# The first microseconds of a layer norm, windowed attention and gated FFN kernel: load order, statistics engine, early tiles and placement of the attention-value runs

## The chip, the cores and the metric

The kernel runs on one core of one Trainium2 chip. The metric is device time in microseconds (us) for one execution. The time before is the median of three runs; one further execution was profiled, and its trace is what the prediction reads.

## The reference

The input x has 2048 rows of 576 features, in bf16. The reference, cut to what matters:

```python
xn = layernorm(x)                            # per row, eps = 1e-5
qkv = xn @ wqkv                              # 576 x 1728; 32 heads of 18
scores = q @ k.T * 18 ** -0.5                # causal, window of 256 keys
s = (softmax(masked scores) @ v) @ wo        # 576 x 576
h = sigmoid(xn @ w_gate) * (xn @ w_up)       # 576 -> 4608
g = silu(h @ w_down)                         # 4608 -> 576
out = x + s * g
```

## The kernel before

**Tiling.** The rows are cut into four chunks of 512 (`NC`), and each chunk into four blocks of 128 rows (`BPC`). A chunk has its layer norm (`build_ln`), its query, key and value projections, attention in eight groups of four heads (`build_attn`), the product with the attention's output matrix (`build_wo`), and the FFN (`build_ffn`): 36 F tiles of 128 columns with gate and up together, called f1, and then the down products, called f2. Contractions of 64 rows run as two matmuls at a time, one in the upper and one in the lower half of the array; "a pair" below is such a couple. The 576 features are 64 (the remainder, held in `wgr`) and four times 128 (in `wgs`). One F tile is a lo half of 4 pairs, which needs `wgs` of gate and of up, and a hi half of 5 pairs, which needs `wgr` as well. A hi half waits for its lo half.

**Order.** Every engine runs a list of operations that a planner in the program (`schedule`) writes out from estimated durations, priorities and memory that comes free. TensorE is filled throughout: FFN tiles are put between the scores of the attention (`space`), so that the exponentials keep up. The FFN uses PSUM units 2, 3 and 1 (`pool_f`), scores, transposes and projections 0 and 1 (`pool_s`). The attention-value products come in eight runs, two to a chunk (`build_pv`), each of 256 (chunk 0) or 384 very short TensorE instructions with all four PSUM units held. `fits` lets a run start only where, by the plan, a stretch of TensorE's instruction list (pages of 256 instructions) has taken long enough before it (`FETCH_NS`).

**The opening.** All loads are issued by SyncE (SP) one after the other: four x blocks, then gate and up columns of the first two F tiles (weights group 0), then the remainder rows for four F tiles, then weights group 1, and so on. Meanwhile TensorE runs matmuls on zeros (`warm`: 43 pairs, and 10 more after the first transposes). For blocks 0, 1 and 3, VectorE takes the sums (L541, L543), aggregates them (L545), adds eps (L547), GpSimd raises to the power of -1/2 (L549), VectorE applies (L557) and copies 64 columns (L561), TensorE transposes (L613), and ScalarE, or VectorE for block 3, copies the result into `xnT` (L590). For block 2 the sums are taken on ScalarE in two passes (L600, L602), with a GpSimd step after each (L601, L603).

**Early tiles.** The first two F tiles (`NEARLY`) are cut by block into four parts of 128 rows, so that TensorE can start on a block as soon as it is there; the lo half of the third tile, whole, runs before the last part's hi half (`ahead`). Three lines that the change rewrites:

```python
pr = 1 + wg if c == 0 and wg < 4 else 3
ahead = self.pool_f.hold()
if edge > at and when(edge) - when(edge - FETCH - FETCH_AHEAD) < FETCH_NS[ffn]:
    return False
```

Of the kernel before, what the change touches and what calls it, by code (L numbers as in the profile page):

```python
# [21 lines left out]
FG = 4  # L22
# [23 lines left out]
FETCH_NS = (6200.0, 4350.0)  # L46
RUN_NS = 6.3
STEP_NS = (54.0, 30.6)
# [20 lines left out]
LN_PRIO = (0, 0, 0, 16)  # L69
X_PRIO = (0, 0, 0, 0)  # L70
REM_PRIO = 0.6
STATS_ACT = (2,)
APPLY_ACT = ()
DUP_ACT = ()
XE_ENG = ("ACT", "ACT", "ACT", "DVE")
NWARM = (43, 10)
NEARLY = 2
FIRST_SLACK_NS = (-800.0, -1500.0)
BUSY_SLACK_NS = 1500.0
PARTS = (((0, 1), (1, 2), (2, 3), (3, 4)),) * NEARLY  # L80
# [10 lines left out]
POOL_IN_NS = 140.0  # L91
DMA_PE_NS = 690.0
FILL_NS = 100.0
SPACE_NS = (1700, 1800, 1700, 1700)
# [8 lines left out]
def act_ns(n):  # L103
    return n / 1.2 + 175.0
# [52 lines left out]
class Pool:  # L157
# [12 lines left out]
    def pick(self, n, now, barred=()):  # L170
        free = []
        for u in self.units:
            if u in barred:
                continue
            h = self.last[u]
            if h is None:
                free.append((0.0, self.units.index(u), u))
            elif h.rel and all(r.idx >= 0 for r in h.rel):
                free.append((max(now, max(r.end for r in h.rel) + self.late), self.units.index(u), u))
# [4 lines left out]
        return max(g[0] for g in got), sorted(g[2] for g in got)  # L184
# [11 lines left out]
class Op:  # L196
    __slots__ = ("eng", "est", "deps", "fn", "name", "prio", "start", "end", "tok", "needs_tok",
                 "nbytes", "slack", "idx", "succs", "cidx", "odeps", "acq", "lane", "filler", "space", "ni", "run", "then")

    def __init__(self, eng, est, fn, name, deps, prio, nbytes, odeps, acq):  # L200
# [33 lines left out]
        self.then = None  # L234
        for d in self.odeps:
            assert d.eng == eng
# [22 lines left out]
class Builder:  # L259
# [40 lines left out]
    def alloc_memory(self):  # L300
# [61 lines left out]
        self.pool_f = Pool("F", [2, 3, 1], last)  # L362
        self.pool_v = Pool("V", [0, 1, 2, 3], last)
# [54 lines left out]
    def load_x(self, c, i=0):  # L418
        if c == 0:
            for i in range(BPC):  # L420
                self.x_dma[i] = (self.dma(self.x0[:, i, :], self.x[i * P:(i + 1) * P, :], P * D * 2, f"dma:x{i}", ("x0", i), prio=X_PRIO[i]),
                                 self.x0[:, i, :])
                self.x_dma[i][0].slack = -220.0
            return
# [11 lines left out]
        for j in range(2):  # L436
            self.x_dma[st + j] = (o, self.xnr[:, slots[j], RD:XW])
# [10 lines left out]
    def build_consts(self):  # L448
# [15 lines left out]
        self.warm(NWARM[0], z, None, 107)  # L464
# [25 lines left out]
    def warm(self, n, dep, before, est):  # L490
        h, zero = self.warm_h, self.warm_src

        def f_warm(eng):
            return pair(eng, self.halves(h, P), lambda r, t: zero[r, :],
                        lambda r, t: zero[r, :], True, True)
        for i in range(n):
            w = self.op("PE", est, f_warm, f"warm:{i}", deps=[dep], prio=4, acq=None if before else h, odeps=[before], ni=4)
            w.filler = h
            h.release(w)
            before = w  # L500
# [24 lines left out]
    def build_ln(self, c):  # L525
# [3 lines left out]
        for i in range(BPC):  # L529
# [10 lines left out]
            else:  # L540
                b1 = op("DVE", 390, lambda e, ss=ss, x_in=x_in: e.bn_stats(self.bnst[:, ss, 0, :], x_in[:, 0:288]),  # L541
                        f"ln:bn1:{st}", deps=[o_x, ds], prio=pr)
                b2 = op("DVE", 390, lambda e, ss=ss, x_in=x_in: e.bn_stats(self.bnst[:, ss, 1, :], x_in[:, 288:576]),  # L543
                        f"ln:bn2:{st}", deps=[o_x, ds], prio=pr)
                ag = op("DVE", 200, lambda e, ss=ss: e.bn_aggr(self.mv[:, ss, :], self.bnst[:, ss, :, :]),  # L545
                        f"ln:ag:{st}", deps=[b1, b2], prio=pr)
                ve = op("DVE", 140, lambda e, ss=ss: e.tensor_scalar(self.veps[:, ss, :], self.mv[:, ss, 1:2], EPS, None,  # L547
                                                                    ALU.add), f"ln:ve:{st}", deps=[ag], prio=pr)
                rs = op("POOL", 560, lambda e, ss=ss: e.tensor_tensor(self.rstd[:, ss, :], self.veps[:, ss, :],  # L549
# [792 lines left out]
```

## Time and profile before

| what | value |
|---|---|
| median of three runs | 557.37 us (556.61 to 557.46) |
| the profiled execution's own time | 556.48 us |
| its span | 555.2 us |
| TensorE (PE) busy | 549.9 us, 99% |
| VectorE, ScalarE, GpSimd busy | 59%, 49%, 38% |
| first matmul with weights | 7.98 us after the span's start |
| instruction queue | 66 packets, 1.08 MB |

The span leaves out 1.28 us of the execution's own time. PE's busy time counts each matmul to its modelled end, so that small gaps do not show in it; they are read from the starts of the matmuls.

### The profile page before, as it was taken

What the parts mean: (1) busy time and instruction counts of PE and PEld (TensorE: products, weight loads), DVE (VectorE), ACT (ScalarE), POOL (GpSimd) and SP (SyncE); (2) the same over time, 40 slices, a digit from 0 to 9 for tenths busy, and PEclk for the clock granted to TensorE, in tenths of its full rate; (3) what the DMA queues carried; (4) which work ended last, traced back from release to release, by engine and by line L of the source; (5) the groups of instructions that cost most, each with busy time, mean ns of one, the idle gap of its engine ahead of it and who ended that gap; (6) DMA issues with size and microseconds to landing.
All of it is one profiled execution on the core that took longest, in us unless ns stands there. A gap on an engine that the chain in (4) does not pass through costs nothing.

```text
span 555.2 us, 19412 instructions
## 1 busy us (share of the span) xinstructions
PE 549.9 (99%) x8342; PEld 341.2 (61%) x8342; DVE 325.1 (59%) x782; ACT 271.7 (49%) x379; POOL 208.8 (38%) x360
## 2 busy tenths in 40 slices
PE   8999999999999999999999999999999999999998
PEld 7454455777555655577855565447877655445887
DVE  5467677745966545746565557664455657653511
ACT  4246554432566543645265563764165555765021
POOL 5634353826271230554452322745063332700300
DMA  8899999542256664462126653663013464540001
GB/s 230 234 263 239 248 241 257 150 91 59 72 164 182 198 167 132 129 161 53 32 65 193 201 162 101 185 179 87 9 34 103 119 204 138 153 134 2 20 28 46
DMA packets 141213, 75.87 MB, mean 137 GB/s; under 512 B 43676, under 2 KB 139260, under 8 KB 141128
## 3 DMA queue, kind: packets, MB, share of 16 engines
q1 hardware_dynamic: 133704, 68.71, 47.3%
q0 software_dynamic: 7424, 5.92, 4.0%
q8 instruction: 66, 1.08, 0.8%
q14 instruction: 19, 0.16, 0.1%
HBM read 63.18 MB, written 2.36 MB: 118 GB/s over the span
## 4 chain that ended last, share of the span: by engine, by line
PE 98%; DMA 1%; SPq 0%; issue 0%; DVE 0%; ACT 0%
PE ps L127 95%; PE ps L817 3%; DMA wgs<-in_B_w_up_dram 1%; SPq L290 0%; ACT thf L1087 0%; PE ps L613 0%; DVE thf L1089 0%; DVE xf L1092 0%
## 5 line engine op out<-in xcount | busy, mean ns | idle before, releaser
L127 PE MATMUL ps<-xnT,wgs 64*128 64x512 bf16 (+1 forms) x2400 | 284.0, 368 | 0.6 <-DMA wgs<-in_B_w_up_dram 0.5
L767 ACT ACTIVATE expr<-ps 128x1024 bf16<-128x1024 f32 (+4 forms) x160 | 155.0, 968 | 81.0 <-PE ps L127 80.5
L127 PEld LDWEIGHTS ps<-xnT,wgs 64*128 64x128 bf16 x2400 | 114.7, 94 | 108.6 <-issue 1.1
L127 PE MATMUL ps<-wd_sb,hT 64*128 64x288 bf16 (+2 forms) x2448 | 152.7, 276 | 0.0
L290 POOL DMA_DIRECT2D qk<-qd x160 | 82.9, 524 | 161.7 <-PE ps L127 152.9
L977 DVE SCALAR_TENSOR_TENSOR hT<-tring,ps 128x512 bf16<-128x512 bf16 x144 | 98.6, 685 | 74.2 <-ACT tring L974 72.6
L974 ACT ACTIVATE tring<-ps 128x512 bf16<-128x512 f32 x144 | 86.2, 598 | 113.9 <-PE ps L127 112.3
L127 PEld LDWEIGHTS ps<-wd_sb,hT 64*128 64x128 bf16 x2448 | 113.0, 94 | 29.4
L780 DVE TENSOR_TENSOR expr<-expr,mask 128x128 bf16<-128x128 bf16 (+2 forms) x240 | 65.2, 299 | 62.0 <-ACT expr L767 59.4
L290 POOL DMA_DIRECT2D oT<-o2T x72 | 36.8, 520 | 115.3 <-DVE ot L848 52.4
L731 POOL TENSOR_SCALAR kx<-kprev,small 128x256 bf16<-128x256 bf16 x64 | 60.1, 949 | 6.0 <-PE ps L127 5.1
L127 PE MATMUL ps<-qk,kx 64*128 64x320 bf16 (+1 forms) x704 | 59.2, 254 | 0.0
L127 PE MATMUL ps<-xnT,wgr 64*128 64x512 bf16 (+1 forms) x300 | 56.0, 367 | 0.0
L127 PEld LDWEIGHTS ps<-qk,kx 64*128 64x128 bf16 x704 | 31.9, 94 | 26.6
L127 PE MATMUL ps<-xnT,wqg 64*128 64x512 bf16 (+1 forms) x320 | 37.7, 355 | 0.0
L652 DVE CAST qd<-ps 128x1024 bf16<-128x1024 f32 (+1 forms) x20 | 22.3, 1115 | 11.1 <-PE ps L127 11.1
L845 DVE STREAM_TRANSPOSE ot<-ps 128x512 f32<-128x512 f32 x32 | 20.3, 687 | 13.9 <-PE ps L817 13.8
L127 PEld LDWEIGHTS ps<-xnT,wgr 64*128 64x128 bf16 x300 | 15.0, 94 | 16.4
L731 DVE TENSOR_SCALAR kx<-qk,small 128x512 bf16<-128x512 bf16 x64 | 21.9, 370 | 5.4 <-PE ps L127 4.9
L853 DVE STREAM_TRANSPOSE o2T<-o 128x512 bf16<-128x512 bf16 x32 | 22.6, 706 | 3.0 <-DMA oT<-o2T 2.5
L127 PEld LDWEIGHTS ps<-xnT,wqg 64*128 64x128 bf16 x320 | 15.0, 94 | 11.5 <-issue 0.4
L1080 ACT ACTIVATE thf<-ps 128x576 bf16<-128x576 f32 x12 | 7.8, 650 | 27.4 <-PE ps L127 27.4
(68 smaller groups left out, 289.3 us busy)
## 6 DMA issues: line engine op xcount, KB each, us to landing
wgs<-in_B_w_gate_dram SPq DMA_DIRECT2D x72, 256.0 KB, 3.5
wgs<-in_B_w_up_dram SPq DMA_DIRECT2D x72, 256.0 KB, 4.0
wd_sb<-in_B_w_down_dram SPq DMA_DIRECT2D x9, 576.0 KB, 6.7
wqg<-in_A_wqkv_dram SPq DMA_DIRECT2D x32, 128.0 KB, 3.8
qk<-qd POOLq DMA_DIRECT2D x100, 36.0 KB, 2.7
wgr<-in_B_w_gate_dram SPq DMA_DIRECT2D x36, 64.0 KB, 3.1
wgr<-in_B_w_up_dram SPq DMA_DIRECT2D x36, 64.0 KB, 2.9
wvo<-in_A_wqkv_dram SPq DMA_DIRECT2D x4, 576.0 KB, 4.2
```

What stands on the lines that cost most here:

```text
L127: res = eng.matmul(outs[i], lhs(ROWS[t], i), rhs(ROWS[t], i), start=start, stop=stop, tile_position=(64 * t, 0))
L290: o = self.op(eng, DMA_ISSUE_NS[eng], lambda e: e.dma_start(dst, src), name, deps, prio, nbytes=nbytes)
L652: return eng.tensor_copy(dst, self.both(h, n))
L731: return e.tensor_scalar(self.kx[:, sx, pos:pos + n_ // SW, t, :], src.rearrange("p (s k) -> p s k", k=SW), self.half[:, t:t + 1], None, A ...
L767: return eng.activation(self.expr[:, se, :, lo * SW:NT], self.both(h, NT)[:, :, lo * SW:NT], ACTF.Exp, scale=SM_SCALE)
L780: return eng.tensor_tensor(e_, e_, m_, ALU.mult)
L817: res = eng.matmul(outs[i][p0:p0 + VH, cols], self.v_aug[ROWS[i], o:o + VH], self.expr[ROWS[i], se, t, cols], start=m == 0, stop=m == len( ...
L845: return e.transpose(self.ot1[:, p1, :], self.halves(hp, NT, un)[i])
L853: t2 = op("DVE", dve_ns(NT), lambda e, p2=p2, p3=p3: e.transpose(self.o2T[:, p3, :], self.o2[:, p2, :]), f"ot2:{c}:{pr}:{i}", deps=[on, d3 ...
L974: th = op("ACT", act_ns(NT), lambda e: e.activation(self.tring[:, st, :], bank(h, 0), ACTF.Tanh, scale=0.5), f"th:{c}:{ft}", deps=[pg, dt_ ...
L977: mu = op("DVE", dve_ns(NT), lambda e: e.scalar_tensor_tensor(self.hT[:, ft, :], self.tring[:, st, :], 1.0, bank(h, 1), ALU.add, ALU.mult) ...
L1080: th = op("ACT", act_ns(w), lambda e: e.activation(v2(t), y2(), ACTF.Tanh, scale=0.25), f"fth:{nm}", deps=[f2, dt_], prio=0)
```

## The change

The fourth x block is issued behind the first gate and up weights. The remainder rows of weights group 0 are loaded alone, for two F tiles, and those of group 1 come as two transfers of their own behind group 1's weights. In chunk 0 the separate VectorE step that adds eps goes: GpSimd adds eps times 576 to the first half's sum of squares while VectorE takes the second half's. Block 1, not block 2, has its sums on ScalarE, and the second ScalarE pass reads the first one's sum directly, without a GpSimd step between them. Block 2's copy into `xnT` goes from ScalarE to VectorE. Three F tiles are early: two in four parts, the third in parts of three blocks and one, and the tile that runs ahead uses PSUM unit 0. The warm-up is 40 pairs, and nothing after the first transposes. In the planner, transfers of the opening have their own latencies, scores are spaced by 1600, 2100, 1700 and 1700 ns (1700, 1800, 1700, 1700 before), and `fits` measures the time for a page of instructions in another way, with a factor for each run.

```diff
-FETCH_NS = (6200.0, 4350.0)
+FETCH_LEAD = 16
+QUEUED = 48
+FETCH_NS = (7300.0, 5500.0, 4250.0)
+RUN_NEED = (1.2, 1.0, 1.1, 1.0, 1.1, 0.95, 1.05, 1.1)
+RELAX_NS = 250e3
-X_PRIO = (0, 0, 0, 0)
+X_PRIO = (0.0, 0.1, 0.2, 1.5)
 REM_PRIO = 0.6
-STATS_ACT = (2,)
+REM1_PRIO = 1.5
+STATS_ACT = (1,)
-XE_ENG = ("ACT", "ACT", "ACT", "DVE")
-NWARM = (43, 10)
-NEARLY = 2
+XE_ENG = ('ACT','ACT','DVE','DVE')
+NWARM = ((40,1),)
+NEARLY = 3
-PARTS = (((0, 1), (1, 2), (2, 3), (3, 4)),) * NEARLY
+PARTS = (((0, 1), (1, 2), (2, 3), (3, 4)),) * 2 + (((0, 3), (3, 4)),)
-POOL_IN_NS = 140.0
+POOL_IN_NS = 100.0
-FILL_NS = 100.0
-SPACE_NS = (1700, 1800, 1700, 1700)
+FILL_NS = 160.0
+SPACE_NS = (1600, 2100, 1700, 1700)
...
+        self.pool_a = Pool("F", [0], last)
...
-                b1 = op("DVE", 390, lambda e, ss=ss, x_in=x_in: e.bn_stats(self.bnst[:, ss, 0, :], x_in[:, 0:288]),
...
-                ve = op("DVE", 140, lambda e, ss=ss: e.tensor_scalar(self.veps[:, ss, :], self.mv[:, ss, 1:2], EPS, None,
-                                                                    ALU.add), f"ln:ve:{st}", deps=[ag], prio=pr)
...
+                if c == 0:
+                    b1 = op("POOL", 230, lambda e, bs=bs: e.tensor_scalar(bs[:, 0, 2:3], bs[:, 0, 2:3], EPS * D, None, ALU.add), f"ln:ep:{st}",
+                            deps=[b1], prio=pr)
+                ag = ve = op("DVE", 210, lambda e, ss=ss, bs=bs: e.bn_aggr(self.mv[:, ss, :], bs), f"ln:ag:{st}", deps=[b1, b2], prio=pr)
+                if c:
+                    ve = op("DVE", 140, lambda e, var=var: e.tensor_scalar(var, var, EPS, None, ALU.add), f"ln:ve:{st}", deps=[ag], prio=pr)
...
-            if i == 0:
-                self.warm(NWARM[1], None, tr, 80)
...
-        m = op("POOL", 150, lambda e: e.tensor_scalar(nm, sx, -1.0 / D, None, ALU.mult), "ln:am", deps=[a1], prio=pr)
-        a2 = op("ACT", act_ns(D) + 150, lambda e: e.activation(junk, x_in, ACTF.Square, bias=nm, accum_out=sq), "ln:aq", deps=[m], prio=pr)
+        a2 = op("ACT", act_ns(D) + 290, lambda e: e.activation(junk, x_in, ACTF.Square, bias=sx, scale=float(D), accum_out=sq), "ln:aq", deps=[a1], prio=pr)
+        m = op("POOL", 230, lambda e: e.tensor_scalar(nm, sx, 1.0 / D, None, ALU.mult), "ln:am", deps=[a1], prio=pr)
...
-                self.op_wgr[wg] = self.load_rem(self.wgr[:, sr, :], (self.wg[:, f8], self.wu[:, f8]), f"dma:wgr:{c}:{wg}",
-                                                ("wgr", sr), pr + (REM_PRIO if c == 0 and wg == 0 else -0.5), [dr])
+                first = c == 0 and wg == 0
+                self.op_wgr[wg], self.op_wgr[wg + 1] = [
+                    self.load_rem(self.wgr[:, sr, a * P:b * P], [w[:, f8][:, a * P:b * P] for w in (self.wg, self.wu)], f"dma:wgr:{c}:{wg}:{a}",
+                                  ("wgr", sr, a), pr + late, [dr])
+                    for a, b, late in (((0, WG, REM_PRIO), (WG, 2 * WG, REM1_PRIO)) if first else ((0, 2 * WG, -0.5),))] * (1 if first else 2)
...
-                        ahead = self.pool_f.hold()
+                        ahead = (self.pool_a if NEARLY > 2 else self.pool_f).hold()
...
-    def fits(self, at, n, st, places, ffn):
+    def fits(self, at, o, st, places, now, rate, waited):
+        n = o.run
+        need = RUN_NEED[sum(int(v) << 1 - j for j, v in enumerate(o.name.split(":")[1:3]))]
...
         edge = at + (FETCH_AT - at) % FETCH
         while edge - FETCH - FETCH_AHEAD < at + n:
-            if edge > at and when(edge) - when(edge - FETCH - FETCH_AHEAD) < FETCH_NS[ffn]:
+            p = edge - FETCH - FETCH_LEAD
+            t0, kind = when(p - QUEUED)
+            for a0, _, _, _, held in reversed(places):
+                if a0 < p - FETCH:
+                    break
+                if a0 <= p:
+                    t0 = max(t0, held)
+            if p >= at:
+                t0 = max(t0, st)
+            if edge > at and when(edge)[0] - t0 < FETCH_NS[kind] * (need - waited / RELAX_NS):
                 return False
             edge += FETCH
```

More of the change, by code (lines that the diff above doesn't have):

```diff
@@ L1162, in schedule @@
                     st = max(free[e], ready_t[o.cidx])
-                    if o.run and not self.fits(at + len(self.new_waits(o, known)) // 2, o.run, st, places, int(ffn[phase] < FETCH)):
+                    if o.run and not self.fits(at + len(self.new_waits(o, known)) // 2, o, st, places, kind, STEP_NS[ffn[phase] < FETCH], st - ready_t[o.cidx]):
                         continue
@@ L1208, in schedule @@
                 at += len(waits) // 2
-                places.append((at, stt, o.est / o.ni))
+                places.append((at, stt, o.est / o.ni, kind, stt if o.run else held))
                 at += o.ni
```

125 lines of the change are left out of this document (72 added, 53 removed).

## The prediction

> **What bounds the kernel now.** I read the page first, then the chain of waits, then the timeline of the opening, the landings of its transfers, and last the starts of TensorE's (PE's) matmuls one by one.
>
> ```profile
> span 555.2 us, 19412 instructions
> ...
> PE 549.9 (99%) x8342; PEld 341.2 (61%) x8342; DVE 325.1 (59%) x782; ACT 271.7 (49%) x379; POOL 208.8 (38%) x360
> ...
> PE 98%; DMA 1%; SPq 0%; issue 0%; DVE 0%; ACT 0%
> ```
>
> PE is the bound. Only three things can shorten the span: an earlier start of real work, a gap on PE that goes, or fewer matmuls. The chain shows where the gaps are:
>
> ```profile
> 3.14 4.71 DMA wgs<-in_B_w_up_dram
> 7.84 0.14 issue
> 7.98 1.00 PE ps L127 x26
> ...
> 86.18 2.07 PE ps L127 x17
> 88.25 0.05 issue
> ...
> 336.28 1.48 PE ps L817 x100
> 337.75 0.09 issue
> 337.84 1.06 PE ps L817 x77
> ```
>
> Real work starts when the first up weights have landed (7.84). From there to 552.7 us I went through every pair of matmuls: a pair of 512 columns takes 216.3 ns, one of 128 takes 58.6, and over 0.09 us beyond the usual distance is lost at few places. They are 0.11 us at 8.4 (below), 0.235 us at 87.85 after the first attention-value run, about 0.1 us at the entry of each of the eight runs, two of 0.1 us at 190.5 and 427, and one gap inside a run, by this timeline of PE:
>
> ```profile
> 336.21 2.69 PE L817 MATMUL ps<-expr,v_aug 64*19 64x320 bf16 x192
> ...
> 395.54 2.47 PE L817 MATMUL ps<-expr,v_aug 64*19 64x320 bf16 x192
> ```
>
> The run at 336 (the fifth of eight) is 0.22 us longer than its like. Just before it the instruction queue moves a 16 KB packet, 0.75 us before the run starts; the other runs have the last packet 1.45 to 3.24 us ahead.
>
> **The change, part by part.**
>
> *Loads.* The landings, from issue plus time to landing: x 2.86, 4.00, 4.56, 4.93; gate 7.12; up 7.84; the two remainders 8.16 and 8.35. DMA is at 0.91 to 0.96 busy and 256 to 269 GB/s in these stretches, so that bytes decide. The fourth block is 147 KB: behind the weights it brings up forward by 147/265 = 0.55 us, to about 7.3. The remainder pair stays behind both, so only its own halving counts: 66 KB less, 0.25 us, 8.35 to 8.10.
>
> *First work on PE.* Today the two lo halves of block 0 start at 7.98, take 8 pairs of 58 ns, and the first hi half waits for the remainder: that is the 0.11 us at 8.4. After the change the lo halves run from about 7.4 to 7.9, and the hi half still starts only behind the remainder, about 8.20 where it was 8.45. So 0.25 us is the gain, not 0.55: the new stall is the remainder's. Bounds: nothing (if the slowest ring, a microsecond behind the others on these loads, does not follow the bytes) to 0.55.
>
> *Block 1 on ScalarE.* From 4.00: pass one 0.77 (4.58 to 5.35 in the trace), pass two 0.87 (5.72 to 6.59), 0.06 between; GpSimd 0.28 and 0.55; VectorE 0.43 and 0.18; transposes 0.32; ScalarE's copy 0.70; with handoffs of 0.03 to 0.10, `xnT` at 8.5, up to 8.8 if block 2's power comes first on GpSimd. Today it is 8.24, on VectorE. PE wants it after both hi halves, 8.20 + 10 x 0.0586 = 8.79. It costs nothing, but the cover is under 0.3 us, and what is missing stalls PE one for one, at most 0.4.
>
> *Eps on GpSimd.* It takes 0.15 us plus a handoff (3.98 to 4.22) off each VectorE chain, and adds a GpSimd step of 0.23 (the row of L601) beside the second half's sums of 0.44. Block 0 has been waiting for weights anyway (`xnT` 7.17 against 7.84): nothing. The aggregate now waits for GpSimd; queued behind it on VectorE are block 0's apply and block 2's sums, and I take 0 to 0.2 us, off the path.
>
> *Blocks 2 and 3.* Block 2, on VectorE from 4.56, should be ready by about 9.1 instead of 9.88; PE takes it at 8.79 + 1.05 + 0.15 = 9.99. Block 3 lands at about 7.84, then its sums, aggregate, power, apply, copies and transposes (0.9, 0.2, 0.55, 0.6, 0.3, 0.5 and handoffs) end at 11.3, or 12.3 if block 2's apply and copies (1.1) go first. Today it is 11.11, and used at 11.45. The third early tile covers it: PE has 1.05 + 0.15 of block 2 and then nine pairs of 384 columns (164 ns by the slope between 128 and 512), so block 3 is wanted at 12.66. Group 1's weights (10.47 today, about the same after, as the bytes ahead are the same up to the half remainder) are wanted at 11.2. Splitting that tile costs 9 x (164 + 58.6 - 216.3) = 0.05 us.
>
> *Two more issues on SP* (0.58 and 0.60, rows of the first remainders) push everything behind them back by up to 1.2 us: group 2's weights (12.44, wanted near 16) and the first query weights (wanted at 20.1). Hidden.
>
> *Warm-up.* Ten pairs of 56 ns lay in an idle stretch: nothing, while the clock stays up. Below is what it costs if it does not.
>
> *Runs.* I take the 0.22 us inside the fifth run as gone, since a run that is held until the page is there has other tiles to put ahead of it; bounds 0 (it moves to another run) to -0.46 (the 0.235 us after the first run goes too). That gap looks like a hi half directly behind its lo half, so spacing alone need not mend it. The Trainium skill ("Runtime: NRT & Kernel Launch", section "Instruction fetch mechanics") has the instructions refilled in blocks of 16 KiB, 256 instructions, and the crossing "mostly hidden"; the trace agrees on the size (66 packets, 1.08 MB) and shows 0.22 us that is not hidden. By that rule alone the whole change would come to 557.17.
>
> Sum on the profiled execution: 556.48 - 0.25 + 0.05 - 0.22 = 556.06. The median of the runs lies 0.89 above that execution, and I carry this offset: 556.95, rounded to 556.9.
>
> **The rivals.**
>
> *Faster.* The 0.89 us between the profiled execution and the median may itself be waits for instructions: four runs that stall as the fifth did make 0.9. The runs at 215, 267 and 395 have their last packet only 1.45, 1.56 and 1.67 us ahead, against 0.75 where it stalled, so a packet late by 0.7 us would stall them. If holding the runs ends these too, 557.37 - 0.42 - 0.89 = 556.06. Against it: no run but the fifth shows a stall in the trace, and the 0.89 may be something else.
>
> *Slower: the clock.* The trace's first matmuls come at half rate until 4.36 us, 3.3 us after the first:
>
> ```profile
> 3.00:4.00 1.00, 1.00 (x24) 1.00 0.92 242
> ...
> 4.43:4.93 0.50, 0.50 (x24) 1.00 0.92 270
> ```
>
> 24 matmuls take 1.0 us and later 0.5 (the column behind them, the granted clock, says 1.00 in both). Today PE's longest gap before real work is 0.98 us. Without the ten pairs it stands from about 5.5 to 7.4, 1.9 us, with half as much before it. If it falls back to half rate and needs as long again as at the start, 3.3 us of work takes 1.65 us more: 557.37 - 0.42 + 1.65 = 558.6. It decides once the half rate lasts 3.1 us or more. The Trainium skill ("TensorE: Matmul & The Clock Gate", Part 1) has the clock drop after an idle window of about 3.4 us; the trace shows no such drop, its longest gap being 0.98 us, and by that rule 1.9 us would be safe unless the few transposes count as idle.
>
> *Slower: the new order.* Scores of chunk 1 are spaced by 2100 ns instead of 1800, and every later place moves. Each hi half that comes directly behind its lo half costs 0.235 us, the row at 87.85. Seven such places make 1.65 us: 558.6 again. Two only take the gain back.
>
> *No gain in the opening.* Block 1 late by 0.25 us, or the remainder no earlier, takes back the first term: 557.2.
>
> **How the numbers follow.** About 0.2% (1.1 us) is what a measurement of this kernel can tell from no change. The forecast (556.9) has 0.32, the opening without gain (557.2) 0.18: both are within 0.2%, together 0.50. Waits gone in the unprofiled runs (556.06) has 0.30: faster by over 0.2%. The clock has 0.12 and the new order 0.08: slower, 0.20. The likeliest is 556.9. The range reaches down to 555.8, the faster case with the 0.235 us gone too, and up to 558.6, where the two slower cases begin to lie half outside. The likeliest one's own range is 556.4 to 557.4.
>
> **What would show it.** First matmul with weights near 7.4, first hi half near 8.2, and an idle PE between the two for want of `wgr`; `xnT` of block 1 near 8.5 and of block 3 after 11.3; pairs of 128 columns at 58 ns from the start (107 would be the clock); eight runs of which none is longer than 1.80 and 2.40 us. It is wrong if real work starts later than 7.98, if PE waits for block 1 or 3, or if new gaps of 0.2 us stand between 15 and 550 us.

## The result and the profile after

The changed kernel takes 559.51 us, the median of 14 runs (557.98 to 564.21), against 556.87 us (556.30 to 557.68, 14 runs) for the kernel before. The ratio is 1.0064, with an interval of 1.0046 to 1.0083. It is slower, outside the predicted range, and its runs lie much further apart. The profiled execution took 563.84 us, at the upper end of them.

The page of the changed kernel, the lines that answer to those of before:

```profile
span 562.6 us, 19413 instructions
...
PE 552.9 (98%) x8334; PEld 345.6 (61%) x8334; DVE 324.7 (58%) x780; ACT 273.0 (49%) x378; POOL 211.2 (38%) x363
...
PEclk9999999899999999999999999999999999999999
...
PE 96%; DMA 2%; SPq 1%; DVE 0%; issue 0%; ACT 0%; POOL 0%; DVEq 0%
```

PE is still the bound, but transfers (DMA) and SP's queue (SPq) now hold 3% of the chain, and one of the 40 slices of the granted clock is not full (slice 8, 98 to 113 us). The chain of waits says where. Its columns are start, length and what held:

```profile
6.06 0.71 ACT xnT L602
6.77 0.05 issue
6.82 1.04 PE ps L139 x16
...
97.75 0.51 SPq L303
98.30 0.52 SPq L303
98.86 7.00 DMA wd_sb<-in_B_w_down_dram
105.86 0.14 issue
106.00 39.23 PE ps L139 x582
...
450.93 1.47 PE ps L829 x99
452.40 0.71 issue
453.11 1.06 PE ps L829 x78
```

Real work starts at 6.82, 1.16 us earlier than before. It is no longer held by weights, which landed at 6.44, but by ScalarE's copy of block 0 into `xnT`, which ends at 6.77. At 106.00 the chain runs through a load of down weights, issued by SP at 98.86. At 452.40 the seventh attention-value run stops for 0.71 us with nothing that the profile shows.

From the start of every matmul I worked out the time lost up to a moment: its start, less the useful matmuls before it at the distance of the full clock (56 ns for a pair of 128 columns, 216 for 512). A wait counts whole in the stretch in which it begins. In us, after against before:

```
up to      before   after    after - before, in this stretch
 15 us      7.89     8.30    +0.41   opening
 90 us      8.42     9.04    +0.21
100 us      8.41     9.34    +0.31
104 us      8.41    13.31    +3.97   wait for the down weights
110 us      8.40    14.82    +1.52   half clock behind that wait
440 us      9.49    15.51    -0.40
460 us      9.51    16.45    +0.92   seventh run
556 us      9.67    16.73    +0.12
```

The sum is 7.06; another 0.3 lies behind the last matmul. The profiled execution is a bad one: 5.49 of it is one wait and the half clock behind it, which do not strike every run alike. So the experiments had to tell three losses apart: the late load (theory A), the opening and its clock (B), and the runs' stalls for instructions (C; in the expectations below C' and F put the seventh run's stall down to SP's loads, G to GpSimd's moves, E and H to the place of the instructions in their page of 256).

### The profile page after: what moved, and what is told of

Read it like the earlier page. It is cut to its first block, busy times and chain, and to the rows that moved or that the text cites. A ratio compares the mean times of both kernels' runs of the same rounds, so it can differ in the third digit from the quotient of the medians.

```text
span 562.6 us, 19413 instructions
## 1 busy us (share of the span) xinstructions
PE 552.9 (98%) x8334; PEld 345.6 (61%) x8334; DVE 324.7 (58%) x780; ACT 273.0 (49%) x378; POOL 211.2 (38%) x363
## 3 DMA queue, kind: packets, MB, share of 16 engines
q8 instruction: 66, 1.08, 0.8%
## 4 chain that ended last, share of the span: by engine, by line
PE 96%; DMA 2%; SPq 1%; DVE 0%; issue 0%; ACT 0%; POOL 0%; DVEq 0%
PE ps L139 93%; PE ps L829 3%; DMA wd_sb<-in_B_w_down_dram 1%; SPq L303 1%; DMA x<-in_A_x_dram 0%; PE ps L625 0%; DVE small L561 0%; ACT xnT L602 0%; POOL small L570 0%; DVE xnr L577 0%; ACT thf L1105 0%; DVE thf L1107 0%; DVE xf L1110 0%; DVE small L567 0%; DVE xnr L581 0%
## 5 line engine op out<-in xcount | busy, mean ns | idle before, releaser
L139 PE MATMUL ps<-xnT,wgs 64*128 64x512 bf16 (+2 forms) x2416 | 284.7, 368 | 1.3 <-ACT xnT L602 0.8
L139 PE MATMUL ps<-wd_sb,hT 64*128 64x288 bf16 (+2 forms) x2448 | 156.0, 277 | 3.8 <-DMA wd_sb<-in_B_w_down_dram 3.8
L139 PEld LDWEIGHTS ps<-wd_sb,hT 64*128 64x128 bf16 x2448 | 116.1, 95 | 31.5 <-issue 4.1
L792 DVE TENSOR_TENSOR expr<-expr,mask 128x128 bf16<-128x128 bf16 (+2 forms) x240 | 64.0, 294 | 79.2 <-ACT expr L779 78.1
L139 PE MATMUL ps<-xnT,wgr 64*128 64x512 bf16 (+2 forms) x302 | 56.3, 367 | 0.0
L570 POOL TENSOR_TENSOR small<-small 128x1 f32<-128x1 f32 x15 | 8.6, 576 | 31.6 <-DVE small L569 29.5
```

Source lines behind the costliest of these rows:

```text
L139: res = eng.matmul(outs[i], lhs(ROWS[t], i), rhs(ROWS[t], i), start=start, stop=stop, tile_position=(64 * t, 0))
L570: rs = op("POOL", 560, lambda e, ss=ss, var=var: e.tensor_tensor(self.rstd[:, ss, :], var, self.neghalf[:, :], ALU.pow), f"ln:rs:{st}", de ...
L792: return eng.tensor_tensor(e_, e_, m_, ALU.mult)
```

## The experiments

Each ran against the kernel before on the same chip (medians 556.54 to 556.73). "Swap" below is one edit to SP's list, made after the plan is finished, so that no other engine's order moves:

```diff
         self.prog = prog
+        sp = prog["SP"]
+        last = self.op_wd[-1]
+        sp.remove(last)
+        sp.insert(next(i for i, o in enumerate(sp) if o.name == "dma:wq:1:1:0"), last)
```

### The late load

**e1, the changed kernel again**, no edit.

> The changed kernel as it is, to see which of its losses come back. Theory A (late load): the first attention-value run is held back from 84 to 97 us, the FFN's f1 tiles run out 1.7 us earlier, and the last load of w_down, issued 9 us later than before, is waited for: 1 to 5 us of idle PE near 102 us in this execution too, and about 559.5 us in the median. Theory B (warm-up): without the ten pairs behind the first transposes the clock sometimes comes up only at 10 us: the loss before 15 us is then 8.3 us, and 7.0 to 7.4 in executions where it came up in time. Rival C (waits for instructions): gaps of 0.2 to 0.9 us inside attention-value runs, at the same run each time (the seventh).

Measured: 558.82 us (556.86 to 563.21), ratio 1.0052 (1.0029 to 1.0075). In this profiled execution (span 556.6) SP issued the same load at 95.29 instead of 98.86, and it landed at 101.03. By the starts of the matmuls PE lost 0.24 us for it, not the 1 to 5 us that theory A expected here; the execution took 557.82, and the others went up to 563.21.

**e2, swap alone.**

> The changed kernel; on SP's list alone the last load of w_down is put ahead of the second group of query weights for chunk 1. All other lists are the same. Theory A: the wait near 102 us is gone or under 0.5 us, and 2 to 4 us with it: 555.8 to 557.5 us. If the clock at the opening (B) or waits for instructions (C) are the cause: 559 to 560 us as before the edit.

Measured: 557.55 us (556.61 to 558.86), ratio 1.0015 (1.0007 to 1.0023). SP's timeline, first of the kernel before, then of the changed kernel and of e2 (start, length, operation):

```profile
89.88 0.48 SPq L290 DMA_DIRECT2D wd_sb<-in_B_w_down_dram  x1
```

```profile
91.93 1.83 SPq L303 DMA_DIRECT2D wqg<-in_A_wqkv_dram  x2
93.80 3.27 SPq L303 DMA_DIRECT2D wqgr<-in_A_wqkv_dram  x1
97.12 0.59 SPq L303 DMA_DIRECT2D wgs<-in_B_w_gate_dram  x1
...
98.86 0.59 SPq L303 DMA_DIRECT2D wd_sb<-in_B_w_down_dram  x1
```

```profile
90.79 0.99 SPq L303 DMA_DIRECT2D wd_sb<-in_B_w_down_dram  x1
91.83 2.43 SPq L303 DMA_DIRECT2D wqg<-in_A_wqkv_dram  x2
94.30 0.89 SPq L303 DMA_DIRECT2D wqgr<-in_A_wqkv_dram  x1
```

In the changed kernel the load stands behind issues that themselves wait (3.27 us in one of them). It holds the rows of the last four of the 36 F tiles, so that the down products come to it after 64 matmuls. In PE's timeline, before and then in the changed kernel, that is at 102.31 and behind the row of 99.57, at 102.0:

```profile
102.31 2.12 PE L127 MATMUL ps<-wd_sb,hT 64*128 64x288 bf16 x32
```

```profile
99.57 2.62 PE L139 MATMUL ps<-wd_sb,hT 64*128 64x288 bf16 x40
106.00 1.15 PE L139 MATMUL ps<-wd_sb,hT 64*128 64x288 bf16 x8 [3.80 <-DMA wd_sb<-in_B_w_down_dram]
```

A transfer of 576 KB took 7.0 us both times (6.4 is the page's median). Before, the load had landed at 96.90, 5.4 us ahead of its use; now it lands at 105.86. So the time of use hardly moved, and the issue moved by 9 us. Issued early enough, the wait is gone, and so are all times over 559. By the ratios of e1 and e2 the late load is worth 0.37%, 2.1 us; by their medians 1.3. Theory A holds, for the larger part of the loss and for nearly all of the scatter.

### The placing rule

**e3, the kernel before with the new rule of `fits` and its constants, and nothing else of the change.**

```diff
-            if edge > at and when(edge) - when(edge - FETCH - FETCH_AHEAD) < FETCH_NS[ffn]:
+            p = edge - FETCH - FETCH_LEAD
+            t0, kind = when(p - QUEUED)
...
+            if edge > at and when(edge)[0] - t0 < FETCH_NS[kind] * (need - waited / RELAX_NS):
```

> The kernel before, with the new rule for placing the runs alone (fits, its constants and what the planner keeps for it); opening, warm-up and spacing as before. The plan then holds the first run back to about 97 us too, but has the last w_down load on SP 6 us earlier than the changed kernel has it. Theory A: holding alone does little as long as the load is early: wait under 1 us, 556.5 to 558 us. Rival D, that the held run itself is the cause (everything behind it late): 559 us or more. If the rule does what it is for, no run is longer than 1.80 (chunk 0) or 2.41 us.

Measured: 559.87 us (559.52 to 560.90), ratio 1.0055 (1.0043 to 1.0067): the rule alone costs 3.2 us, where I expected almost nothing. PE's timeline of e3:

```profile
145.12 1.83 PE L821 MATMUL ps<-expr,v_aug 64*19 64x320 bf16 x122
147.81 0.21 PE L821 MATMUL ps<-expr,v_aug 64*19 64x64 bf16 x6 [0.86 <-issue]
```

The second run, 1.79 us long before, takes 2.83; the fifth takes 2.88 (2.63 before). The last run starts at 522.3 instead of 513.2, and 4.8 us lie between the last matmul and the end, 2.7 before. Of the 3.4 us by which this profiled execution is longer than the one before, 1.3 lie in these two runs and 2.1 at the end. The size is the one that rival D gave, and it came without a wait for down weights; that the late runs cause the longer end was not tested by itself. So the rule doesn't end the stalls. It moves them, and the order with them.

**e12, the changed kernel with the old rule.** The edit is the reverse of e3's in `fits`, with `FETCH_NS` of before.

> The changed kernel with the old rule for placing the runs (fits and its constants), the rest of the change kept: opening, warm-up, spacing of scores. The plan has the first run at 86 us, f1's end at 97.2, the last w_down load two microseconds earlier than wanted instead of late. Theory A: no wait of over 1 us near 100 us and no upper tail. The plan itself ends 2.9 us later than the changed kernel's (attention of chunk 1 spread over the wider spacing), so 558.5 to 561 us all the same. Rival: if the rule is the whole cost of the change, 556 to 557 us.

Measured: 562.87 us (562.17 to 563.38), ratio 1.0109 (1.0093 to 1.0124), worse than either. There is no wait for down weights (the first run is back at 87.75), but the sixth run stalls by 2.11 us and the eighth by 0.69:

```profile
381.52 1.82 PE L829 MATMUL ps<-expr,v_aug 64*19 64x320 bf16 x138
385.20 0.89 PE L829 MATMUL ps<-expr,v_aug 64*19 64x256 bf16 x54 [1.87 <-issue]
```

Another 1.3 us gap stands at 131, where PE waits for an exponential. So the old rule serves the order of the other edits worse than the new one does; which of these edits moves the order most was not tried one by one.

### The opening and its clock

**e4, swap, and ten warm-up pairs behind the first transposes again, planned with the rest.**

```diff
             self.r_xn.release(sn, tr)
+            if i == 0:
+                self.warm(10, 1, None, tr, 80)
```

> The changed kernel with the last w_down load early as in the run beside it, and with ten warm-up pairs again behind the first transposes (the plan is made anew with them, so the runs move by up to 2 us). Theories A and B together: no wait near 102, full clock before 8 us, loss before 15 us of 7.0 to 7.5: 555.5 to 556.5 us. If the ten pairs do nothing, the same time as with the load alone.

Measured: 559.28 us (558.25 to 559.93), ratio 1.0040 (1.0028 to 1.0052). The clock was up early, but the ten pairs changed the plan: the fifth run stalls by 1.08 us, and two gaps of 0.55 and 0.36 stand at 11 and 17. The expectation missed since I took the order as fixed. The later edits were therefore made after the plan.

**e6, swap, and the 40 warm-up pairs with 8 columns instead of 128**, so that the clock has no cause to come up before real work.

```diff
+        def f_small(eng):
+            return pair(eng, self.halves(h, 8), lambda r, t: zero[r, :], lambda r, t: zero[r, 0:8], True, True)
-            w = self.op("PE", wide * est, f_warm, ...
+            w = self.op("PE", wide * est, f_small, ...
```

> The kernel with the last w_down load early; the forty warm-up pairs stream 8 columns each instead of 128, so that the array is nearly idle until 6.9 us. All lists and places of instructions are the same. Theory B: the clock comes up only after the real work has begun, at 9 to 11 us in every execution: loss before 15 us of 8.3 to 8.6 us, 0.2 to 0.6 us more in the median than with the early load alone: 557.7 to 558.2. If the warm-up does not matter: 557.5 with a loss of 7.7.

Measured: 558.35 us (557.89 to 559.16), ratio 1.0031 (1.0021 to 1.0041), 0.8 above e2.

**e7, swap, and ten of the 40 pairs moved behind the first transposes after the plan, ten others with 256 columns.**

```diff
+        late = [o for o in pe if o.filler is not None][30:40]
+        for o in late:
+            pe.remove(o)
+        at_tr = next(i for i, o in enumerate(pe) if o.name == "tr:0") + 1
+        pe[at_tr:at_tr] = late
...
+            w = self.op("PE", wide * est, f_wide if 20 <= i < 30 else f_warm, ...
```

> The kernel with the last w_down load early; of the forty warm-up pairs ten go behind the first transposes, and ten of the thirty left are made twice as long (256 columns), so that the first part lasts as long as before and the number and places of all instructions behind are the same. Theory B: the clock comes up before 7 us in every execution: loss before 15 us near 7.7 us, 0.2 to 0.4 us less in the median than with the early load alone: 557.1 to 557.4, with less spread. Otherwise the same time, 557.5.

Measured: 557.33 us (556.41 to 558.43), ratio 1.0012 (1.0004 to 1.0021), 0.2 below e2 although the seventh run stalls by 1.66 in its profiled execution (1.31 in e2's).

How the clock goes is read from the matmuls of 128 columns in a microsecond. Windows of PE: the stretch, its length, PE's busy time and matmuls, the granted clock, DMA's share and GB/s. First the changed kernel, then e1, then e14 (told below):

```profile
7.00:8.00 1.00, 1.00 (x28) 1.00 0.97 279
8.00:9.00 1.00, 1.00 (x28) 1.00 0.87 248
...
108.00:109.00 1.00, 1.00 (x12) 0.50 0.02 2
```

```profile
7.00:8.00 1.00, 1.00 (x45) 1.00 0.97 288
8.00:9.00 1.00, 0.91 (x38) 1.00 0.86 230
```

```profile
7.00:8.00 1.00, 0.94 (x35) 0.87 1.10 327
8.00:9.00 1.00, 1.00 (x28) 0.50 0.67 190
```

The same opening goes three ways. The clock never comes up before real work, and pairs take 107 ns until 10.2 to 10.5 us (28 to 30 matmuls in a microsecond: the changed kernel, e2, e12, e13, and by intent e6). It comes up between 3.9 and 7.0 and stays (45: e1, e4, e5, e7 to e11, e15, e18). Or it comes up and falls back at 7.1 to 8.4, with the granted clock at 0.50, until 10.5 to 11.8 (e14, e16, e17). The time lost up to 15 us is 8.3 to 8.6 in the first case, 7.05 to 7.73 in the second (7.94 and 8.13 in e4 and e18, which have other waits besides) and 8.2 to 9.35 in the third, against 7.89 before. Every profile of a kernel with pairs behind the first transposes (e4, e7, e8, e11, e15, e18) is of the second kind. All executions bear this out. A mean granted clock of 0.997 over 557 us is one stretch of 3.41 us at half rate; 21 of the 68 executions of e2, e5, e9, e10, e13, e14, e16 and e17 show it, but none of the 60 with pairs behind the first transposes.

What goes with these three can be read from the traces' own records of the granted clock, which all profiles but those of before and e1 hold. Every change in them lies on a grid of 3.41 us, whose place differs from execution to execution (e14: 4.33, 7.75, 11.16). PE's busy share of each stretch of this grid, by the profile, goes with what the clock does at its end:

```
at half rate   76% or less     stays at half rate   (after 3.33 to 6.75: 76%; e8 0.21 to 3.62: 75%)
at half rate   78% or more     comes up             (e17 0.29 to 3.71: 78%; e7 0.49 to 3.90: 84%)
at full rate   49% or less     falls                (e17 3.71 to 7.12: 43%; e14 4.33 to 7.75: 49%)
at full rate   53% or more     stays                (e10 4.33 to 7.75: 53%; e9 4.53 to 7.94: 57%)
```

So a warm-up without a break from 1.05 to 5.3 us can fail, when the grid cuts it into two stretches of which neither is full: that is the changed kernel's profile. And e14 and e10 have the same grid and nearly the same gap; work began at 7.06 in the one and at 6.87 in the other, and only e14 falls at 7.75. So the new opening is mostly worth 0.15 to 0.85 us with the clock up, and costs 0.3 to 1.5 without it; and the new warm-up doesn't secure the clock: by these profiles it depends on where the grid lies, which no run here could set.

### The seventh run

In the changed order the seventh run stalls by 0.84 to 1.7 us in every profiled execution (e4 and e12, planned anew, have other orders). Its place in the list is new; the runs below take the suspects one at a time.

**e5, swap, and two weight loads of 256 KB that SP issues just ahead of the run held until its first half is done.**

```diff
+        run = next(o for o in prog["PE"] if o.name == "pv:3:0:0")
+        for o in sp:
+            if o.name == "dma:w:3:5:0":
+                o.deps.append(run)
```

> The kernel with the last w_down load early, and besides the two 256 KB weight loads that are issued 1.6 and 0.9 us ahead of the seventh attention-value run now wait on SP until the run's first half has ended. TensorE's list is the same. Theory C': the page of instructions comes late because these loads are ahead of it in the DMA rings: the packet then starts over 1 us before the run, the run takes 2.40 us and not 3.7, and the whole 556.0 to 556.5 us, 1.3 less than with the early load alone. Rival: the page is late because of what PE did before (the place of the run); then the run keeps its 0.8 to 1.4 us and the time is 557.5.

Measured: 557.56 us (556.22 to 558.17), ratio 1.0010 (1.0001 to 1.0018). The run still stalls, by 1.44.

**e8, e5 and e7 together.**

> The changed kernel with all three: last w_down load early, the two weight loads held until the seventh run is half over, ten of the warm-up pairs behind the first transposes. If theories A, B and C' are right: loss before 15 us of 7.7, no wait near 100 us, no run over 2.41 us: 555.6 to 556.1 us, less than the kernel before (556.65).

Measured: 556.79 us (556.34 to 557.76), ratio 1.0003 (0.9994 to 1.0012), level with the kernel before. The stall is 0.84. No other variant of the change came out lower.

**e9, swap and one more warm-up pair; e10, swap and one pair fewer**, so that all later instructions of TensorE move by four places to either side.

```diff
+        more = copy.copy(pe[5])
+        more.needs_tok = False
+        pe.insert(5, more)
```

> The kernel with the last w_down load early, and one more warm-up pair at the start, which moves every later TensorE instruction by four places within its page of 256. Nothing else changes. Theory E (place): PE is held by VectorE until 1.36 us before the seventh run, at an instruction that lies a few places too early in its page for the sequencer's reading ahead to reach the page's end; so the next page is asked for only when the hold ends, and its packet starts 1.0 to 2.1 us after that. Four places later the end is within reach at the hold before: packet 2 us ahead of the run, run of 2.40 us, and the whole 1.0 to 1.4 us less than with the load alone: 556.1 to 556.6. If transfers or the time before the run decide: the stall of 0.8 to 1.7 us stays, 557.5.

> The same kernel with one warm-up pair less: every later TensorE instruction four places earlier in its page. Theory E: the seventh run keeps its stall, and the third and fifth, which now start at place 221 of a page where the seventh starts at 222, fall back to 217 and stall as well, each by 0.5 to 1.7 us: 558.5 to 560 us. If the place does not matter: 557.5, one run stalling.

Measured: e9 557.70 us (556.47 to 558.85), ratio 1.0016 (1.0007 to 1.0025); e10 558.16 (557.59 to 558.85), 1.0027 (1.0015 to 1.0038). The run stalls by 1.67 and 1.66.

**e11, swap, e7's warm-up and e9's pair.**

> Last w_down load early, ten of the warm-up pairs behind the first transposes (with the twenty longer columns ahead), and one more warm-up pair: the three repairs that theories A, B and E give. Loss before 15 us of 7.0 to 7.7, no wait near 100 us, eight runs without a stall: 555.5 to 556.1 us, 0.6 to 1.1 under the kernel before. If E falls: 557.3.

Measured: 557.52 us (557.10 to 558.10), ratio 1.0014 (1.0005 to 1.0023); the stall is 1.67.

**e13, swap, and all four loads that SP issues in the 2.7 us ahead of the run held**: as e5, with `"dma:wgr:3:4:0"` added. **e14, swap, and four moves that GpSimd issues ahead of the run put three operations later. e15, both, with e7's warm-up.**

```diff
+        moves = [o for o in pl if o.name in ["dma:sp:3:%d:0:3" % u for u in (24, 25, 26, 27)]]
+        for o in moves:
+            pl.remove(o)
+        n = next(i for i, o in enumerate(pl) if o.name == "kp:3:5") + 1
+        pl[n:n] = moves
```

> The kernel with the last w_down load early, and all four SP loads that are issued from 2.7 us ahead of the seventh run on (two of 64 KB, two of 256 KB) wait until the run's first half has ended. In the two runs looked at that do not stall, the page's packet started within 0.5 us of the end of a burst of transfers; in the seventh it starts as the two 64 KB loads end. Theory F (queue behind loads): the packet starts 1 us or more ahead of the run and the stall falls from 0.8 to 1.7 us to under 0.4; 556.2 to 556.8 us. If GpSimd's four moves ahead of them hold it (G), or PE itself, the stall stays.

> The kernel with the last w_down load early, and on GpSimd's list alone the four moves of queries and keys that are issued 4.4 to 2.3 us ahead of the seventh run are put behind the three operations after them, so that they start at the run. They are wanted 13 us later. Theory G (the page waits for GpSimd's moves, the only thing that the seventh run has ahead of it and the third and fifth have not): the packet starts 2 us ahead of the run, no stall; 556.1 to 556.6 us. Theory F: the stall stays.

> Everything that has a reason: last w_down load early, the four SP loads held, the four moves put back, ten of the warm-up pairs behind the first transposes. If F or G is right, the seventh run takes 2.40 us, the loss before 15 us is 7.0 to 7.7 and the time 555.6 to 556.2 us, under the kernel before (556.6). If neither: 557.3.

Measured: e13 557.13 us (556.67 to 558.05), ratio 1.0012 (1.0003 to 1.0020), stall 1.02; e14 559.77 (557.74 to 561.54), 1.0050 (1.0031 to 1.0068), stall 1.00; e15 557.03 (556.51 to 558.37), 1.0009 (1.0001 to 1.0018), stall 1.38. In e13 no transfer is under way in the last microsecond before the run, and still the packet of instructions starts only 0.16 us ahead of it. So the packet isn't slowed by other transfers; it starts late. Why e14's median is 2.2 us above e2's was not settled: its profiled execution, at 557.89, is one of its two lowest, is below e2's (558.10), and so doesn't show the loss.

**e16 and e17, swap and five pairs more or fewer**, 20 places to either side; **e18, e16 with e7's warm-up.**

> The changed kernel with the last down weights issued ahead of a load that the plan has before them (as e2), and five more warm-up pairs, so that every later TensorE instruction stands 20 places further back in the program. Theory H (the packet of instructions for the seventh run is asked for only when TensorE passes its wait for VectorE 1.36 us ahead of the run, because a boundary of the instruction buffer lies just behind that wait): 20 places are more than the few instructions between the boundary and the wait, so the seventh run's stall of 1.31 us shrinks to under 0.3, and the time is about 556.3. Rival (the place in the buffer does not matter; one or four places made no difference): the seventh run still stalls by 1 or more, and the time is 557.3 to 557.9.

> As e16 but with five warm-up pairs fewer than the changed kernel, so that every later TensorE instruction stands 20 places further forward. Theory H: the boundary moves to the other side, the seventh run's stall changes by over 0.8 or another run (the third or the fifth) stalls in its place. Rival: the seventh run stalls by 1 to 1.4 as in e2, and the time is 557.5 to 558.3, the longer opening clock included.

> As e16, and ten warm-up pairs stand behind the first transposes and ten of the others have 256 columns (as e7). If theory H holds, the time is 555.6 to 556.2, below the kernel before (about 556.6); by its rival 557.0 to 557.5, as e7.

Measured: e16 559.27 us (557.52 to 559.30), ratio 1.0035 (1.0022 to 1.0048); e17 558.98 (558.48 to 561.45), 1.0050 (1.0035 to 1.0064); e18 557.56 (556.48 to 559.08), 1.0014 (1.0005 to 1.0023). The stalls are 1.25, 1.36 and 1.52; in e17 the fourth and the sixth run stall too, by 0.33 and 0.78. Theory H in its simple form falls. PE's timeline of e2, then of e16:

```profile
443.13 1.89 PE L139 MATMUL ps<-xnT,wgs 64*128 64x512 bf16 x16
444.95 1.56 PE L829 MATMUL ps<-expr,v_aug 64*19 64x320 bf16 x114
447.67 0.60 PE L829 MATMUL ps<-expr,v_aug 64*19 64x64 bf16 x38 [1.15 <-issue]
```

```profile
444.28 1.89 PE L139 MATMUL ps<-xnT,wgs 64*128 64x512 bf16 x16
446.10 1.48 PE L829 MATMUL ps<-expr,v_aug 64*19 64x320 bf16 x104
448.61 1.20 PE L829 MATMUL ps<-expr,v_aug 64*19 64x192 bf16 x88 [1.03 <-issue]
```

Twenty instructions more ahead of the run, and the stop comes exactly ten matmuls (with ten weight loads) earlier; in e17 it comes ten later, and two to either side in e9 and e10. So TensorE runs out at the end of a page. The shift moves where the page ends, and not when the next one is fetched.

What does go with the packet's start is a wait. Ahead of the third, fifth and seventh runs, in e3 of the second and in e12 of the eighth, PE has a wait for VectorE (where a tile takes over a PSUM unit). Times before the run's start, in us; the third column says how long VectorE's write had ended when PE came through:

```
kernel, run     wait for VectorE   written since   packet starts   stall
before, 7th         -2.84              0.47           -1.82         0
before, 5th         -2.41              0.03           -0.74         0.22
e3, 5th             -2.41              0.03           -0.78         0.49
after, 5th          -3.71              0.46           -2.34         0
after, 7th          -1.33              0.03           -0.10         0.84
e2, 7th             -1.33              0.03           -0.19         1.31
e13, 7th            -1.33              0.03           -0.16         1.02
e16, 7th            -1.33              0.03           +0.05         1.25
e3, 2nd             -1.43              0.03           +0.03         1.04
e4, 5th             -1.34              0.03           +0.15         1.08
e12, 8th            -3.50              0.03           -0.32         0.69
```

In the 58 such places of the 19 profiles without e12 the packet starts 0.94 to 2.04 us behind the wait, 1.40 in the median; in e12's one place it is 3.18. Where the write had ended 0.03 us before, VectorE does hold PE's list; where it had ended 0.17 to 0.47 us before, it does not. All 21 places of the first kind stall, and none of the 38 of the second. VectorE's row shows such a hold. In e2, its write into `hT` ends at 443.58, and PE's wait at 443.62:

```profile
442.89 0.69 DVE L995 SCALAR_TENSOR_TENSOR hT<-tring,ps 128x512 bf16<-128x512 bf16 x1 [1.23 <-ACT tring L992]
```

So in its new place the seventh run has this wait some 24 instructions ahead, and is held by it; the fifth run of the new order has it some 66 ahead, is not held, and doesn't stall. This reading goes with the stalls of the fifth and seventh runs in these 19 profiles, with e3's second and e12's eighth, and with the seventh run's stall staying whatever was done to loads, GpSimd's moves and places. It is a regularity and not a test: an order with another tile ahead of the seventh run was not tried, so that the cause of the late packet is not shown. It doesn't account for the fourth run in e17, nor for the sixth in e12 and e17, nor for the 0.09 us of e12's third, which have no such wait. And since e17's fourth and sixth stall in no other variant of this order, the place in the page is not without effect everywhere.

## Why the prediction was wrong

**Loads: direction right, size wrong.** I had up weights at 7.3 and remainders at 8.10. They landed at 6.44 and at 7.08 and 7.27. The step "bytes decide" at 265 GB/s failed: from 4.0 to 5.5 us the changed kernel's DMA moved 318 to 332 GB/s (277 to 293 in e1), where the one before moved 250 to 276. And bytes were not all that decided. A load reports its landing in 16 parts, and before, the last part of the up weights came 0.88 us behind the fifteenth; now it came 0.28 behind. That is 0.60 of the 1.40 us by which they landed earlier. First work came at 6.82, not 7.4. The wait for `wgr` that I forecast ahead of the first hi half isn't in that profile nor in e1's; in e16, where up weights came late (PE waited 1.11 us for them), it is there with 0.83, and the last part of those remainder rows came 1.06 us behind the fifteenth.

**The opening's new bound was misnamed.** With the clock up (e1), the first hi half ran at 7.72. "It costs nothing" failed for block 1: its copy into `xnT` ended at 8.40, a little earlier than forecast, but PE had finished both hi halves at 8.05 (8.79 in the forecast) and the transposes behind them at 8.20, and went on at 8.46, 0.25 us later. That is the size of the rival "No gain in the opening", and eight of the ten profiles with the clock up have this gap at 0.25 to 0.26. Then PE reached group 1's up weights early, at 9.76, and waited for them until 10.39, by the matmuls' starts 0.63 us. The rows of e1's timeline:

```profile
8.05 0.31 PE L625 MATMUL ps<-ident,xnr 64*128 64x64 bf16 x10
8.46 0.86 PE L139 MATMUL ps<-xnT,wgs 64*128 64x128 bf16 x24
...
10.39 0.83 PE L139 MATMUL ps<-xnT,wgs 64*128 64x384 bf16 x8 [0.47 <-DMA wgs<-in_B_w_up_dram]
```

I had them wanted at 11.2 and landing at 10.47; here they landed at 10.26. So of the 1.09 us by which work began earlier, these two waits took 0.88. The gain was 0.16, near the -0.25 of the sum by luck: an earlier start larger than forecast, and two waits that I had not priced, nearly cancel to it. In the changed kernel's profile block 1 was ready at 8.86 (8.5 to 8.8 forecast); block 3, at 12.96, was later than the 12.3 forecast and missed nothing, because PE at half clock came to it only at 13.07. (A pair of 128 columns takes 0.056 us at the full clock, not the 0.0586 of the sums, which makes 0.03 us on ten pairs.)

**"Nothing, while the clock stays up" was the wrong condition.** The clock rival had its price about right, but I saw only one form of it, the fall in the gap. That form is in e14, e16 and e17. In the profiled execution of the changed kernel the clock wasn't up to begin with: full rate came at 4.36 before and at 10.2 after, although the pairs up to 4.36 are the same in both. Its cost, +0.41 up to 15 us instead of -0.25, is a miss of some 0.7 in those executions. The Trainium skill ("TensorE: Matmul & The Clock Gate", Part 1) says that the clock is judged by a window of about 3.4 us that runs free of the kernel's start, and that an idle one brings the half rate. The records agree with the window's length and with its running free (the grid of 3.41 us), and so does the half clock from 106.0 to 109.2 behind a gap of 3.8 us, which held a whole stretch, 102.32 to 105.73. They do not agree that the window must be idle: in e14 the warm-up ended at 5.0 and work began at 7.06, with ten transposes between, and the rate fell at 7.75 behind a stretch that was 49% busy. So the weighing in the prediction, by which a gap of 1.9 us would be safe unless the few transposes count as idle, asked the wrong question: the stretch need not be idle for the clock to fall.

**"Two more issues on SP ... Hidden" looked at too few loads.** It held for the weights that I named. What I never priced is that re-placing the runs re-writes SP's list too: the issue of the last down weights moved from 89.88 to 98.86, while the work that wants them stayed at 102. This term, absent from the sum, is 1.3 us by the medians of e1 and e2 (2.1 by their ratios) and 5.5 in the profiled execution (3.97 and the half clock behind it). The rival "the new order" had the right sign, but its price was for hi halves behind lo halves, and of gaps of 0.2 us or more between 15 and 90 us there are two new ones (0.24 at 43.5, 0.46 at 71.2, the second for `wgr`).

**"Runs: I take the 0.22 us as gone" failed in size and sign.** The fifth run is indeed 2.40 long now. But the seventh stalls by 0.84 to 1.7 in the place that the rule gave it, and my upper bound was 0, "it moves to another run", at the same size. A stall has no fixed size: it is what the packet is late by. e3 shows that this rule, by itself, costs 3.2 us.

**The offset.** The 0.89 us between the profiled execution and the median was mostly the draw of three runs: over the 14 runs of the result the kernel before has 556.87, and in the later comparisons 556.54 to 556.73, 0.06 to 0.25 above that execution. So the "faster" rival had little to take.

## What to carry to other kernels

Where a planner writes all lists out, a rule that moves one group of instructions re-writes every queue; for each big load, compare the time of issue plus its landing with the time of its first use, in both lists, before counting what the rule saves. Make experiments behind the plan, by moving single entries, since every re-planned variant here (e3, e4, e12) brought losses of its own that were larger than the effect in question. And let warm-up reach up to the first real work: one that ends early costs nothing in some executions and 0.3 to 1.5 us in others, by where the clock's grid lies.

## What the runs showed of the hardware

- **Instructions.** The 16 KB packet of a page of 256 instructions took 0.9 to 1.5 us where a run stopped (1.03 in the median of all packets), but its end is not the end of the wait: in all 25 runs that stopped by 0.09 us or more, of 160, TensorE went on 1.3 to 1.6 us after the packet's end and 2.3 to 3.1 us after its start. No run stalled by more than 0.1 us where the packet started 1.05 us or more ahead of it; with 0.74 to 1.00 the stalls were 0.1 to 0.5, and with less 0.7 to 2.1. The Trainium skill ("Runtime: NRT & Kernel Launch", section "Instruction fetch mechanics") has the crossing "mostly hidden"; in these 25 runs it is not. Where PE has a wait for VectorE ahead of a run, the packet started 0.94 to 2.04 us behind it in 58 of 59 places, in e13 too, where no other transfer was under way in the last microsecond ahead of the run.
- **Clock.** It changes on a grid of 3.41 us. In these profiles it came up behind stretches that were 78% busy or more and not at 76% or less, and fell behind 49% or less and not at 53% or more. The granted clock in the profile shows only a fall (0.50 in e14 at 8 to 9 us); in the changed kernel the same half rate stands beside a granted clock of 1.00, because it had not come up yet. The matmuls' own distance, 107 or 56 ns, tells both.
- **Loads.** With the fourth x block behind the weights, the opening's transfers ran at 318 to 332 GB/s instead of 250 to 276, in the profiled execution, and the last of a weight load's 16 parts, 0.88 to 1.16 us behind the fifteenth in the kernel before, was at most 0.38 behind there. It is not the same in every execution: e1 had 277 to 293, and in e16 the remainder's last part was 1.06 us behind again.
